# Small rows of w_up: ten DMA engines and three column blocks instead of eight engines and two and a half

## The chip, the cores and the metric

The kernel runs on one core of a Trainium2 chip. The core has five engines that work side by side: PE (TensorE, matrix products), DVE (VectorE), ACT (ScalarE), POOL (GpSimd) and SP (SyncE, which here only issues loads). Sixteen DMA engines move data between the chip's memory (HBM) and the core's on-chip memory (SBUF, 128 partitions). The metric is the device time of one execution in microseconds; lower is better.

## The reference

One token `x` of 512 elements goes through two branches, and a gate mixes them. Everything is bf16.

```
q   = x @ wq                      # 32 heads of 128
k,v = the last 4096 of 65536 cached positions, 8 heads, each used by 4 query heads
a   = softmax(q k^T / sqrt(128)) v @ wo
u   = x @ w_up ; gt = x @ w_gate  # both 512 x 1792
b   = (sigmoid(gt) * u) @ w_down  # 1792 x 512
g   = sigmoid(sum(x * gate_w))
out = g * a + (1 - g) * b
```

There is little arithmetic for each byte: the weights and the used part of the caches are 30.67 MB and each byte is read once.

## The kernel before

All large loads are issued by SP, in one queue and in the order of the code: wq (4 MB), eight loads of K (1 MB each, L122), w_gate (L132), w_up (L138 and L144), eight loads of V (L122), two of wo and four of w_down (L109). Up to eight loads are open at a time: a load takes over the semaphore of the one eight places earlier and waits until that one has landed. V loads also wait for the buffers of K, which DVE frees by transposing K (L230). A load is cut into packets that are shared out among DMA engines; each engine adds one to the load's semaphore when its share has landed, and whoever needs the data waits for all of them.

The compute follows the loads. PE projects q (L242), computes the scores S_ps from the transposed K (L269), multiplies w_gate (`glu(0, wg_sb)`), then V by the softmax weights (L344), then w_up (`glu(1, wu_sb)`), then wo and, as the last pieces of w_down come in, w_down (`add_row`, L335). The result row is copied to SBUF by DVE and ACT (L392, L393) and stored (L394). The order on PE, DVE and ACT from L219 on is the order of the code; before that a scheduler sets it.

w_up is a 512 x 1792 matrix. The tile wu_sb puts four consecutive rows (`c` = 0 to 3) on each of the 128 partitions. The main load brings for each partition all but the last FX elements of its four rows. These last elements, of the row `c` = 3, are what this case is about: the "small rows". They are loaded a second way, into the tile wx_sb, by four loads with another shape (L144), so that their 128 packets of 2240 bytes fall on other engines than the rest does:

```python
FX = 5 * FQ // 2          # 1120 columns of the 1792; FQ = 448
wx_v = B_w_up.rearrange("(h b j i c) f -> h b i j c f", h=2, b=2, j=4, i=8)[:, :, :, :, DC - 1, F - FX:F]
```

Each of the four loads brings 32 rows, from a source of 8 by 4 rows. As the small rows lie on other partitions than wu_sb's, the multiplication needs the matching elements of x in the same order. DVE picks them out of the row xr into xp (L195), PE turns xp into a column (xx_ps, L197), and DVE copies it to xx (L202). In `glu(1)` the columns that the main load lacks are then added by two matmuls for each block of columns, one for each half `h` of the small rows (L288).

Of the kernel before, what the change touches and what calls it, by code (L numbers as in the profile page):

```python
# [14 lines left out]
BF16 = mybir.dt.bfloat16  # L15
F32 = mybir.dt.float32
# [3 lines left out]
def kernel(  # L20
# [14 lines left out]
    nc = tc.nc  # L35

    P = 128
    D = A_x.shape[-1]
    DC = D // P
# [8 lines left out]
    F = B_w_gate.shape[1]  # L48
# [3 lines left out]
    FQ = F // 4  # L52
# [12 lines left out]
    const = ctx.enter_context(tc.tile_pool(name="const", bufs=1))  # L65
# [7 lines left out]
    ps_m = ctx.enter_context(tc.tile_pool(name="ps_m", bufs=2, space=bass.MemoryType.PSUM))  # L73

    gap = const.tile([1, 8], F32, name="gap")
    nc.gpsimd.memset(gap[:], 0.0)
    xr = const.tile([1, 2, D], BF16, name="xr")
    nc.scalar.dma_start(xr[:, 0, :], A_x[0, :, :])  # L80
    nc.scalar.dma_start(xr[:, 1, :], gate_w.rearrange("(o n) -> o n", o=1))
# [1 line left out]
    dq = nc.sync  # L83
# [43 lines left out]
    for a in range(HP):  # L127
# [4 lines left out]
    i = dq.dma_start(wg_sb[:].rearrange("p c f -> p (c f)"), B_w_gate.rearrange("(p c) f -> p (c f)", c=DC))  # L132
    reads[i.ins.name] = ((4 * DC * F, P // 4), (1, 4 * DC * F))
    wu_sb = w14.tile([P, DC, F], BF16, name="wu_sb", tag="w14")

    FX = 5 * FQ // 2
    LM = DC * F - FX
    dq.dma_start(wu_sb[:].rearrange("p c f -> p (c f)")[:, 0:LM],  # L138
                 B_w_up.rearrange("(p c) f -> p (c f)", c=DC)[:, 0:LM])
    wx_sb = const.tile([64, 2, 3 * FQ], BF16, name="wx_sb")  # L140
    wx_v = B_w_up.rearrange("(h b j i c) f -> h b i j c f", h=2, b=2, j=4, i=8)[:, :, :, :, DC - 1, F - FX:F]
    for h in range(2):
        for b in range(2):
            dq.dma_start(wx_sb[32 * b:32 * b + 32, h, 0:FX], wx_v[h, b])  # L144

    vv = []
    for a in range(HP):
# [41 lines left out]
    for c in range(DC):  # L189
        nc.tensor.matmul(xt_ps[:, c:c + 1], lhsT=xr[:, 0, c:D:DC], rhs=ident[0:1, 0:1],  # L190
                         start=True, stop=True, skip_group_check=True)
    xx_ps = ps_m.tile([64, 2], F32, name="xx_ps", tag="m")
    xp = const.tile([1, 2, 64], BF16, name="xp")
    for h in range(2):
        nc.vector.tensor_copy(xp[:, h, :].rearrange("o (b i j) -> o b i j", b=2, j=4),  # L195
                              xr[:, 0, :].rearrange("o (h b j i c) -> o h b i j c", h=2, b=2, j=4, i=8)[:, h, :, :, :, DC - 1])
        nc.tensor.matmul(xx_ps[:, h:h + 1], lhsT=xp[:, h, :], rhs=ident[0:1, 0:1],  # L197
                         start=True, stop=True, skip_group_check=True)
    xT = const.tile([P, DC], BF16, name="xT")
    nc.vector.tensor_copy(xT[:], xt_ps[:])  # L200
    xx = const.tile([64, 2], BF16, name="xx")
    nc.vector.tensor_copy(xx[:], xx_ps[:])  # L202


# [18 lines left out]
    for u in range(4):  # L223
        nc.tensor.matmul(S_ps[u // 2][:, u % 2, :], lhsT=other[:].rearrange("p o y u -> p (o y u)"),  # L224
                         rhs=ident[0:2, 0:2].rearrange("p (o y) -> p o y", o=1).to_broadcast([2, 256, 2]),
                         start=True, stop=False)
# [11 lines left out]
    for k in range(8):  # L238
        q_ps = ps_big.tile([P, 512], F32, name="q_ps", tag="b")
        ks = slice(k * 512, (k + 1) * 512)  # L240
        for c in range(DC):
            nc.tensor.matmul(q_ps[:], lhsT=xT[:, c:c + 1].to_broadcast([P, P]),  # L242
                             rhs=wq_sb[:, c, ks], start=(c == 0), stop=(c == DC - 1))
# [18 lines left out]
    for a in range(HP):  # L262
        for v in range(2):
            kT = kTs[a, v] if (a, v) in kTs else k_transpose(a, v)
            k_v = kT[:].rearrange("p (n dhi s t) -> p n dhi s t", n=KB, dhi=2, s=32)
            for dhi in range(2):
                for t in range(2):
                    for hb in range(2):
                        nc.tensor.matmul(S_ps[v][:, hb, :], lhsT=q_st[:, a, dhi, :, t],  # L269
                                         rhs=k_v[:, hb * 16:(hb + 1) * 16, dhi, :, t],  # L270
                                         start=False, stop=(a == HP - 1 and dhi == 1 and t == 1))
# [4 lines left out]
    def glu(w, wsb):  # L276
        for c in range(DC):
            for j in range(4):
                g_out = gu_ps[w][32 * j:32 * j + 32, 0:FQ]

                f0, f1 = j * FQ, (j + 1) * FQ
                fm = min(max(F - FX, f0), f1) if w == 1 and c == DC - 1 else f1
                if fm > f0:
                    nc.tensor.matmul(g_out[:, 0:fm - f0], lhsT=xT[:, c:c + 1].to_broadcast([P, 32]),  # L284
                                     rhs=wsb[:, c, f0:fm], start=(c == 0), stop=(c == DC - 1 and fm == f1))
                if fm < f1:
                    for h in range(2):
                        nc.tensor.matmul(g_out[:, fm - f0:FQ], lhsT=xx[:, h:h + 1].to_broadcast([64, 32]),  # L288
                                         rhs=wx_sb[:, h, fm - (F - FX):f1 - (F - FX)], start=False, stop=(h == 1))


    pm2 = work.tile([P, 2], F32, name="pm2")
    for v in range(2):
        nc.vector.tensor_reduce(pm2[:, v:v + 1], S_ps[v][:].rearrange("p a b -> p (a b)"), axis=AX.X, op=ALU.max)  # L294
    pm = work.tile([P, 1], F32, name="pm")
    nc.vector.tensor_tensor(pm[:], pm2[:, 0:1], pm2[:, 1:2], op=ALU.max)
    glu(0, wg_sb)
    sge = work.tile([P, FQ], F32, name="sge")
    nc.scalar.activation(sge[:], gu_ps[0][:, 0:FQ], AF.Exp, scale=-1.0)  # L299
# [7 lines left out]
                     start=True, stop=True)  # L307
# [34 lines left out]
    for a in range(HP):  # L342
        for m in range(NP // 4):
            nc.tensor.matmul(pv_ps[32 * a:32 * a + 32, :, :],  # L344
                             lhsT=eT[:, a, 4 * m:4 * m + 4, :].rearrange("p n r -> p (n r)"),
                             rhs=vv[a][:, 4 * m:4 * m + 4, :],
                             start=(m == 0), stop=(m == NP // 4 - 1))
# [7 lines left out]


    glu(1, wu_sb)

    o_ps = ps_m.tile([P, HQ], F32, name="o_ps", tag="m")
# [7 lines left out]
    for u in range(2):  # L367
        for t in range(2):
            nc.tensor.matmul(oY_ps[:, 16 * u:16 * u + 16], lhsT=perm[:, u, t, :], rhs=oX[:, 16 * t:16 * t + 16],
                             start=(t == 0), stop=(t == 1))  # L370
# [54 lines left out]
```

## Time and profile before

| what | value |
|---|---|
| median of 7 times | 79.62 us (79.38 to 80.76) |
| the seven times | 79.60, 79.73, 79.49, 80.75, 79.38, 79.62, 80.76 us |
| profiled execution | 79.53 us, of which span 77.9 us |
| PE busy | 51.9 us (67%) |
| DVE busy | 38.3 us (49%) |
| ACT, POOL busy | 10.9 us, 4.6 us |
| mean TensorE clock granted | 0.976 |
| read from HBM | 30.67 MB, 394 GB/s over the span |
| small loads wx_sb | four, 70 KB each, issued 20.3 to 27.6 us |
| `glu(1)` on PE | w_up matmuls 63.6 to 65.3 us, small rows 65.1 to 65.7 us |

The profile gives for every engine its busy time, and for idle time what ended it. A load is followed from its issue to its landing. The "chain that ended last" goes back from the last instruction to what released it, step by step; the DMA view gives the packets of a stretch of time by queue, and a table of stages gives, for chosen stretches, busy time and count of each engine, the granted clock, the mean share of time in which the 16 DMA engines were busy, and GB/s. Beside these views the trace holds every single DMA packet with start, length and size (without the engine's number), and the time of every increment of a load's semaphore.

### The profile page before, as it was taken

The page shows a single profiled execution, that of the slowest core. Times are in us where ns is not written, and L with a number is a line of the kernel's source. Part 1 is how long each engine was busy: PE and PEld are TensorE (multiplying, and loading weights), DVE is VectorE, ACT ScalarE, POOL GpSimd, SP SyncE. Part 2 cuts the span into 40 slices and gives each one's busy share as a digit, 9 for nine tenths or more (in the row PEclk, how much of TensorE's full clock was granted, in tenths as well). Part 3 has the DMA queues.
Part 4 walks back from the last instruction along what each step waited for, and adds up shares of the span by engine and source line. Part 5 has one row for each costly group of instructions (what it writes and reads, how often), then busy time and mean ns, then how long its engine had stood idle before and what let it go on. Part 6 is the DMA issues. An engine that isn't in the chain of part 4 may idle for free.

```text
span 77.9 us, 823 instructions
## 1 busy us (share of the span) xinstructions
PE 51.9 (67%) x318; PEld 23.8 (31%) x318; DVE 38.3 (49%) x49; ACT 10.9 (14%) x20; POOL 4.6 (6%) x18
## 2 busy tenths in 40 slices
PE   0100092999914788988889305999997699576760
PEld 0200041344402233333332202335442244455520
DVE  0600900029959999999995429983000000591020
ACT  2400000337742000000000293000000003000010
POOL 7940020000000000000000000000000000000000
PEclk9999999999999999999999995599999999999999
DMA  5889799898997989996999979989799897998600
GB/s 152 303 353 505 337 505 454 353 505 353 488 471 337 539 353 454 471 471 273 422 500 412 522 303 522 438 370 522 303 522 438 370 522 320 497 438 358 284 32 1
DMA packets 1624, 30.71 MB, mean 394 GB/s; under 512 B 435, under 2 KB 438, under 8 KB 598
## 3 DMA queue, kind: packets, MB, share of 16 engines
q1 hardware_dynamic: 1616, 30.67, 92.6%
q8 instruction: 2, 0.03, 0.2%
q10 hardware_dynamic: 6, 0.00, 0.0%
HBM read 30.67 MB, written 0.00 MB: 394 GB/s over the span
## 4 chain that ended last, share of the span: by engine, by line
DMA 93%; SPq 2%; PE 1%; DVE 1%; issue 0%
DMA wu_sb<-in_B_w_up_dram 30%; DMA wd_sb<-in_B_w_down_dram 27%; DMA kn<-in_A_k_cache_dram 21%; DMA vv<-in_A_v_cache_dram 15%; SPq L122 1%; PE a_ps L335 1%; DVE res L392 1%; SPq L115 0%
## 5 line engine op out<-in xcount | busy, mean ns | idle before, releaser
L269 PE MATMUL S_ps<-kT,qbig 128*128 128x512 bf16 x64 | 15.2, 378 | 5.0 <-DVE qbig L258 2.8
L344 PE MATMUL pv_ps<-vv,eT 128*32 128x512 bf16 x64 | 15.5, 404 | 4.0 <-DVE eT L316 2.8
L230 DVE STREAM_TRANSPOSE kT<-kn 128x2048 f32<-128x2048 f32 x8 | 17.8, 2282 | 0.2 <-DMA kn<-in_A_k_cache_dram 0.2
L269 PEld LDWEIGHTS <-qbig 128*128 128x128 bf16 x64 | 6.1, 97 | 14.1 <-issue 4.2
L344 PEld LDWEIGHTS <-eT 128*32 128x32 bf16 x64 | 6.2, 102 | 12.5 <-issue 3.4
L242 PE MATMUL q_ps<-wq_sb,xT 128*128 128x512 bf16 x32 | 8.6, 436 | 1.4 <-DMA wq_sb<-in_A_wq_dram 1.4
L363 DVE TENSOR_TENSOR oT<-o_ps,rb 128x32 bf16<-128x32 f32 x1 | 0.2, 192 | 13.2 <-PE o_ps L361 13.2
L247 DVE STREAM_TRANSPOSE qtT<-q_sb 128x512 f32<-128x512 f32 x4 | 2.7, 691 | 6.8 <-ACT q_sb L244 6.8
L224 PE MATMUL S_ps<-ident,other 2*128 2x512 bf16 x4 | 2.0, 610 | 5.6 <-DVE other L182 5.6
L244 ACT CAST q_sb<-q_ps 128x512 bf16<-128x512 f32 x8 | 4.7, 586 | 7.0 <-PE q_ps L242 7.0
L242 PEld LDWEIGHTS <-xT 128*128 128x128 bf16 x32 | 3.5, 110 | 6.8 <-issue 4.1
L335 PE MATMUL a_ps<-wo_sb,oY 128*1 128x256 bf16 x64 | 3.8, 272 | 1.3 <-DMA wo_sb<-in_A_wo_dram 1.0
L335 PEld LDWEIGHTS <-oY 128*1 128x1 bf16 x64 | 2.7, 83 | 2.2 <-issue 1.2
L316 DVE STREAM_TRANSPOSE eT<-e_sb 128x1024 bf16<-128x1024 bf16 x2 | 2.4, 1224 | 1.9 <-ACT e_sb L314 1.9
L299 ACT ACTIVATE sge<-gu_ps 128x448 f32<-128x448 f32 x1 | 0.5, 544 | 18.9 <-PE gu_ps L284 18.9
L354 ACT COPY pv_sb<-pv_ps 128x512 f32<-128x512 f32 x1 | 0.6, 586 | 17.3 <-PE pv_ps L344 17.3
L326 DVE RECIPROCAL sg<-sge 128x448 f32<-128x448 f32 x1 | 3.0, 2953 | 0.0
L294 DVE TENSOR_REDUCE pm<-S_ps 128x1 f32<-128x1024 f32 x2 | 2.4, 1208 | 0.9 <-PE S_ps L269 0.9
L392 DVE CAST res<-a_ps 1x256 bf16<-1x256 f32 x1 | 0.4, 413 | 4.9 <-PE a_ps L335 4.9
L207 DVE TENSOR_TENSOR gpr<-xr 1x512 f32<-1x512 bf16 x1 | 0.7, 680 | 4.4 <-DMA xr<-in_gate_w_dram 4.4
L190 PE MATMUL xt_ps<-ident,xr 1*128 1x1 bf16 x4 | 0.3, 165 | 3.5 <-POOL ident L165 3.5
L335 PE MATMUL a_ps<-wd_sb,hT 128*1 128x256 bf16 x28 | 2.0, 271 | 0.7 <-DMA wd_sb<-in_B_w_down_dram 0.5
(64 smaller groups left out, 32.2 us busy)
## 6 DMA issues: line engine op xcount, KB each, us to landing
kn<-in_A_k_cache_dram SPq DMA_DIRECT2D x8, 1024.0 KB, 16.1
vv<-in_A_v_cache_dram SPq DMA_DIRECT2D x8, 1024.0 KB, 12.2
wq_sb<-in_A_wq_dram SPq DMA_DIRECT2D x1, 4096.0 KB, 12.3
wo_sb<-in_A_wo_dram SPq DMA_DIRECT2D x2, 2048.0 KB, 21.3
wg_sb<-in_B_w_gate_dram SPq DMA_DIRECT2D x1, 1792.0 KB, 21.2
wu_sb<-in_B_w_up_dram SPq DMA_DIRECT2D x1, 1512.0 KB, 23.5
wd_sb<-in_B_w_down_dram SPq DMA_DIRECT2D x1, 1024.0 KB, 24.2
wd_sb<-in_B_w_down_dram SPq DMA_DIRECT2D x1, 384.0 KB, 22.7
```

What stands on the lines that cost most here:

```text
L224: nc.tensor.matmul(S_ps[u // 2][:, u % 2, :], lhsT=other[:].rearrange("p o y u -> p (o y u)"), rhs=ident[0:2, 0:2].rearrange("p (o y) -> p ...
L230: nc.vector.transpose(t[:].bitcast(F32), kn[a][:, v * KB:(v + 1) * KB, :] .rearrange("p n d -> p (n d)").bitcast(F32))
L242: nc.tensor.matmul(q_ps[:], lhsT=xT[:, c:c + 1].to_broadcast([P, P]), rhs=wq_sb[:, c, ks], start=(c == 0), stop=(c == DC - 1))
L244: nc.scalar.copy(q_sb[:, ks], q_ps[:])
L247: nc.vector.transpose(qtT[:].bitcast(F32)[:, kq], q_sb[:].bitcast(F32)[:, kq])
L269: nc.tensor.matmul(S_ps[v][:, hb, :], lhsT=q_st[:, a, dhi, :, t], rhs=k_v[:, hb * 16:(hb + 1) * 16, dhi, :, t], start=False, stop=(a == HP ...
L294: nc.vector.tensor_reduce(pm2[:, v:v + 1], S_ps[v][:].rearrange("p a b -> p (a b)"), axis=AX.X, op=ALU.max)
L316: nc.vector.transpose(eT[:, :, v * KB:(v + 1) * KB, :].rearrange("p a n r -> p n a r"), e_sb[:, v, :].rearrange("p (n a r) -> p n a r", a= ...
L326: nc.vector.reciprocal(sg[:], sge[:])
L335: nc.tensor.matmul(a_ps[32 * i:32 * i + 1, i, 0:HN], lhsT=lhsT, rhs=rhs[:, i * HN:(i + 1) * HN], start=start, stop=stop)
L344: nc.tensor.matmul(pv_ps[32 * a:32 * a + 32, :, :], lhsT=eT[:, a, 4 * m:4 * m + 4, :].rearrange("p n r -> p (n r)"), rhs=vv[a][:, 4 * m:4 ...
L392: nc.vector.tensor_copy(res[:, 0:HN], a_ps[0:1, 0, 0:HN])
```

## The change

The small rows become three whole blocks of columns (1344 columns, 2688 bytes a row). The main load becomes shorter to match: 5824 elements a partition for 6048. The four small loads bring 30, 30, 30 and 40 rows, from sources of 10 by 3 and 10 by 4 rows. These are 130 rows: rows 88 and 89 are loaded twice, and their elements of x in the second place are set to zero. wx_sb has 70 partitions for 64; the first half uses 60 of them. The picking of x is now done by DVE (two copies) and POOL (one copy and two memsets), and the two matmuls that turn xp wait for both. In `glu(1)` the block `j` = 0 of `c` = 3 comes whole from wu_sb and the other three from wx_sb: 19 matmuls for 20. The memset of the unused tile `gap` on POOL is taken out.

```diff
-    gap = const.tile([1, 8], F32, name="gap")
-    nc.gpsimd.memset(gap[:], 0.0)
...
-    FX = 5 * FQ // 2
+    WX_PARTS = [(0, 0, 0, 3), (0, 30, 30, 3), (1, 0, 60, 3), (1, 30, 88, 4)]
+    WX_N = [60, 70]
+    FX = 3 * FQ
     LM = DC * F - FX
     dq.dma_start(wu_sb[:].rearrange("p c f -> p (c f)")[:, 0:LM],
                  B_w_up.rearrange("(p c) f -> p (c f)", c=DC)[:, 0:LM])
-    wx_sb = const.tile([64, 2, 3 * FQ], BF16, name="wx_sb")
-    wx_v = B_w_up.rearrange("(h b j i c) f -> h b i j c f", h=2, b=2, j=4, i=8)[:, :, :, :, DC - 1, F - FX:F]
-    for h in range(2):
-        for b in range(2):
-            dq.dma_start(wx_sb[32 * b:32 * b + 32, h, 0:FX], wx_v[h, b])
+    wx_sb = const.tile([70, 2, FX], BF16, name="wx_sb")
+    for h, p0, e0, r in WX_PARTS:
+        dq.dma_start(wx_sb[p0:p0 + 10 * r, h, :], B_w_up[DC * e0:DC * (e0 + 10 * r), :]
+                     .rearrange("(j i c) f -> i j c f", j=r, i=10)[:, :, DC - 1, F - FX:F])
...
-    xx_ps = ps_m.tile([64, 2], F32, name="xx_ps", tag="m")
-    xp = const.tile([1, 2, 64], BF16, name="xp")
+    xx_ps = ps_m.tile([70, 2], F32, name="xx_ps", tag="m")
+    xp = const.tile([1, 2, 70], BF16, name="xp")
+    nc.gpsimd.memset(xp[:, 0, WX_N[0]:WX_N[1]], 0.0)
+    nc.vector.tensor_copy(xp[:, 0, 0:WX_N[0]].rearrange("o (b i j) -> o b i j", b=2, j=3),
+                          xr[:, 0, 0:DC * WX_N[0]].rearrange("o (b j i c) -> o b i j c", b=2, j=3, i=10)[:, :, :, :, DC - 1])
+    for (h, p0, e0, r), eng in zip(WX_PARTS[2:], (nc.gpsimd, nc.vector)):
+        eng.tensor_copy(xp[:, h, p0:p0 + 10 * r].rearrange("o (i j) -> o i j", j=r),
+                        xr[:, 0, DC * e0:DC * (e0 + 10 * r)].rearrange("o (j i c) -> o i j c", j=r, i=10)[:, :, :, DC - 1])
+
+    nc.gpsimd.memset(xp[:, 1, 30:38].rearrange("o (i j) -> o i j", j=4)[:, :, 0], 0.0)
     for h in range(2):
-        nc.vector.tensor_copy(xp[:, h, :].rearrange("o (b i j) -> o b i j", b=2, j=4),
-                              xr[:, 0, :].rearrange("o (h b j i c) -> o h b i j c", h=2, b=2, j=4, i=8)[:, h, :, :, :, DC - 1])
         nc.tensor.matmul(xx_ps[:, h:h + 1], lhsT=xp[:, h, :], rhs=ident[0:1, 0:1],
                          start=True, stop=True, skip_group_check=True)
...
-                f0, f1 = j * FQ, (j + 1) * FQ
-                fm = min(max(F - FX, f0), f1) if w == 1 and c == DC - 1 else f1
-                if fm > f0:
-                    nc.tensor.matmul(g_out[:, 0:fm - f0], lhsT=xT[:, c:c + 1].to_broadcast([P, 32]),
-                                     rhs=wsb[:, c, f0:fm], start=(c == 0), stop=(c == DC - 1 and fm == f1))
-                if fm < f1:
-                    for h in range(2):
-                        nc.tensor.matmul(g_out[:, fm - f0:FQ], lhsT=xx[:, h:h + 1].to_broadcast([64, 32]),
-                                         rhs=wx_sb[:, h, fm - (F - FX):f1 - (F - FX)], start=False, stop=(h == 1))
+                if w == 1 and c == DC - 1 and j >= 1:
+                    for h, n in enumerate(WX_N):
+                        nc.tensor.matmul(g_out, lhsT=xx[0:n, h:h + 1].to_broadcast([n, 32]),
+                                         rhs=wx_sb[0:n, h, (j - 1) * FQ:j * FQ], start=False, stop=(h == 1))
+                    continue
+                nc.tensor.matmul(g_out, lhsT=xT[:, c:c + 1].to_broadcast([P, 32]),
+                                 rhs=wsb[:, c, j * FQ:(j + 1) * FQ], start=(c == 0), stop=(c == DC - 1))
```

In the built program SP still issues four small loads between w_up and V. On POOL, the two memsets and the copy stand after `spare` and before the copies of `perm`. On PE, the two matmuls of xp now stand behind the first matmul of L224, which waits for DVE.

More of the change, by code (lines that the diff above doesn't have):

```diff
@@ L200 @@
     nc.vector.tensor_copy(xT[:], xt_ps[:])
-    xx = const.tile([64, 2], BF16, name="xx")
+    xx = const.tile([70, 2], BF16, name="xx")
     nc.vector.tensor_copy(xx[:], xx_ps[:])
```

## The prediction

> **What bounds the kernel now.** I read the whole page first, then the chain that ended last, the DMA view whole and in two windows, the tiles wu_sb and wx_sb, a table of stages over the end, and the trace's single records: every DMA packet with start, length and size, and every increment that a load makes on its semaphore.
>
> Queues of the whole span (packets, MB, share of 16 engines' time), then the chain by line:
>
> ```profile
> q1 hardware_dynamic: 1616, 30.67, 92.6%
> q8 instruction: 2, 0.03, 0.2%
> ...
> DMA wu_sb<-in_B_w_up_dram 30%; DMA wd_sb<-in_B_w_down_dram 27%; DMA kn<-in_A_k_cache_dram 21%; DMA vv<-in_A_v_cache_dram 15%; SPq L122 1%; PE a_ps L335 1%; DVE res L392 1%; SPq L115 0%
> ```
>
> The load queue is full for 92.6% of the span and carries 93% of the chain. So the question is when the last of the 16 DMA engines finishes its share. The second line will matter: two packets that are no data. The same view in windows 39 to 40.1 us and 67.4 to 68.6 us:
>
> ```profile
> q8 instruction: 1, 0.02, 5.5%
> ...
> q8 instruction: 1, 0.02, 5.1%
> ```
>
> Each is one packet of 16384 bytes, 0.96 and 0.98 us long, on one engine (5.5% of 16 x 1.1 us = 0.97 us).
>
> The end, by stages (last two columns: mean DMA share, GB/s), and the chain there (start, length, what):
>
> ```profile
> 72.80:73.30 0.50, 0.14 (x4) 0.11 (x5) 0.00 (x0) 0.00 (x0) 0.00 (x0) 1.00 0.67 279
> 73.30:74.10 0.80, 0.80 (x18) 0.59 (x16) 0.00 (x0) 0.00 (x0) 0.00 (x0) 1.00 0.53 220
> 74.10:74.70 0.60, 0.48 (x8) 0.24 (x6) 0.00 (x0) 0.00 (x0) 0.00 (x0) 1.00 0.16 62
> ...
> 53.73 20.93 DMA wd_sb<-in_B_w_down_dram
> 74.66 0.04 issue
> 74.70 0.64 PE a_ps L335 x6
> 75.34 0.40 DVE res L392
> ```
>
> The engines do not finish together. The last w_down load makes its 16 increments at 73.15 to 73.65 us (six engines) and at 74.47 to 74.98 us (ten). From 74.98 the tail is fixed: last matmul, copy of res until 75.74, output store, span 77.9; 79.53 with what lies around it, against a median of 79.62 over seven times.
>
> Who are the ten? On each engine one packet starts within 5 ns of the end of the one before, so packets can be strung into 16 chains. A 32768-byte packet takes 1.213 us on every one, so the chains keep the offsets they had when the first load ended (12.09 to 12.69 us). From there to the last packet: six "plain" chains 60.56 us; eight "carriers", which have the small w_up rows, 62.02; two hit by an instruction packet 62.10. So the small rows cost a carrier 1.46 us (sixteen 2240-byte packets of 91 ns, four increments of 9 ns, 0.03 of overlaps) and an instruction packet costs its engine 1.54, of which the trace shows 0.96 to 0.98 for itself and 0.47 to 0.50 more in the data packet after it. The two fall on different engines, and neither is a carrier. In finish times: carriers 74.12 to 74.62, hit engines 74.40 and 74.53, plain 72.80 to 73.29. The kernel is balanced by this: eight engines carry extra so that two hit ones need not.
>
> **What the change does to each kind of engine.**
> 1. Main load of w_up, 11648 for 12096 bytes a partition, eight a partition group, all 16 engines. From 8192 bytes in 309 ns and 12096 in 453 the slope is 0.0369 ns a byte: 16.5 ns less a packet, -0.13 us on every engine.
> 2. Small rows on a carrier: 13 packets of 2688 bytes. From 2240 bytes in 91 ns and 4096 in 159: 107.4 ns. 13 x 107.4 + 4 x 9 - 0.03 = 1.40 us for 1.46. With step 1 an old carrier changes by -0.13 - 0.06 = -0.19.
> 3. Two engines newly carry: -0.13 + 1.40 = +1.27. The number of carriers is the first dimension that both sides share: now 32 rows from 8 by 4 and eight increments a load (the trace counts eight and one immediate); then 30 or 40 rows from 10 by 3 or 4, so ten.
> 4. Other engines: -0.13.
>
> Sum if the two new carriers are plain ones: they end at 72.80..73.29 + 1.27 = 74.07..74.56, old carriers at 74.43, hit engines at 74.27 and 74.40. The last end moves from 74.62 to between 74.43 and 74.56: -0.19 to -0.06 us. If a new carrier is the engine hit at 67.55: 74.53 + 1.27 = 75.80, or +1.18 us; if it is the one hit at 39.07: 74.40 + 1.27 = 75.67, +1.05. Everything behind waits along: the last w_down piece, six matmuls, res, store.
>
> **Which engines are they?** The trace numbers no engines, and this is the unknown that decides. By chance, two of the eight non-carriers miss both hit ones in 15 of 28 pairs. But the first packets of the first load start in an order: seven of eight carriers at 1.759 to 1.846 us, one at 1.901, the non-carriers at 1.885, 1.961, 1.969, 1.986, 1.994, 1.995, 1.998, 2.688. (Two chains that touch within 4 ns are told apart by the lone gate_w packet, which I take to be on a carrier.) Halves so cleanly ordered suggest the engines are started in sequence. The chain that starts at 1.885 is the one hit at 67.55; the one at 1.969 is the one hit at 39.07. If ten engines are the first ten of that sequence, the new carriers are 1.885 and 1.961 or near them: a hit engine among them. I put this at 0.58.
>
> The row: ten-engine loads are not in this trace; eight-engine ones are. [...] The row again: each instruction packet cost its engine 1.54 us here. [...]
>
> **Small steps, and what hides them.**
> - Start: gap's memset leaves (0.10 us), two POOL memsets (0.09 to 0.10 each by spare and gap) and a POOL copy of 30 elements come (between 0.26, the perm copies, and 1.28, DVE's slower xp copy). They stand after spare (ends 3.97) and before the four perm copies, which nobody needs until 67. The DVE xp copies, two of 1.2 us overlapping to 1.32, stay about that.
> - The second wait: both xx matmuls now wait for POOL and are queued behind the first "other" matmul (9.56, 0.60). So xx comes some 0.9 us later, z_ps behind it 0.3 later, then gex and gg; two xx matmuls 0.26. PE's next work, q_ps, waits until 13.06 for wq, after PE stood idle 1.38 us. Hidden; without that cover 0.3 us.
> - glu(1): 19 matmuls for 20, six of them on 60 or 70 rows. At most 0.2 us of PE less at 65, before idle waits of 1.04 (wo) and 0.53 (wd). Nothing.
> - SP: still four small loads. Later V loads reuse their semaphores; a fetch-hit carrier would land them at 41.30 + 1.40 = 42.70 instead of 41.62, while three V loads stay queued until 48.88. Nothing, or below 0.1.
>
> **The rivals.**
> - A, forecast: a hit engine becomes a carrier, +1.05 to +1.18, at the latest chain offset (12.69 for 12.44) +1.43. 79.62 + 1.13 = 80.75. For it: start order. Against: order inside a half may be chance.
> - B, other side: both new carriers are plain. -0.06 to -0.19; 79.43 to 79.56, take 79.48, within 0.3%. It decides as soon as both hit engines are outside the ten. The hit pair then ends last or nearly so. A gain over 0.3% (0.24 us, about what a measurement of this kernel can tell from no change) needs chain offsets luckier than this run's by 0.05 or more: I give that a fourth of B.
> - C: the hit engines differ between executions. Two of the seven times are 80.75 and 80.76, what an instruction packet on a carrier would give (62.02 + 1.54 for the chain, some +1.1 to +1.5). Ten carriers of 16 are then hit more often than eight, and a median falls in the upper or the lower group. No third time comes from it; it raises A against chance, and I count it in A and B.
> - D: the load runs on fewer engines than ten. On five, 26 packets are 2.83 us: carriers +1.24, and 80.9. Price much like A; 0.02.
>
> **How the numbers follow.** A and D 0.60; B 0.40, of which 0.10 beyond 0.3%. The time is A's: 80.75, A's own range 80.5 to 81.05. Both cases must be in the range: 79.38 (B's better end less a little of run-to-run spread) to 81.05 (79.62 + 1.43). Between the two groups I expect little.
>
> **What would show it.** Right in A: last w_down load's increments with one or two alone, over 1 us after the rest; a chain with both a 16384-byte packet and thirteen 2688-byte ones; 107 and 437 ns for the new packets; the six matmuls of the tail starting near 75.9. Right in B: four increments near 73.1 to 73.5, twelve within 74.2 to 74.95. Wrong in both: a last increment later than 76.5, or PE waiting for xx before 13 us. The prediction falls if both instruction packets stay on engines that carry nothing.

## The result, and the profile after

The changed kernel takes 81.21 us as a median of 24 times (79.85 to 82.04), the kernel before 79.63 us over 59 (79.30 to 81.07). The ratio is 1.0088, with a 95% interval of 1.0069 to 1.0106: slower, by less than one per cent. The times of both kernels fall into groups, and the ratio leaves out what lies over 1.5% above a kernel's fastest time, which is 13 of the changed kernel's 24 and its profiled execution too; the plain medians stand at 1.020.

Sorted, the times of the changed kernel are 79.85, 79.86, 79.94; eight from 80.28 to 80.71; nine from 81.18 to 81.49; four from 81.77 to 82.04. Of the kernel before, 14 of 59 lie over 80.5 and the rest within 79.3 to 80.1. The profiled execution of the changed kernel is one of the nine: 81.36 us, span 79.7 (before: 79.53 and 77.9), so its span has 1.8 us to account for.

The chain of waits of the changed kernel, its end (start, length, what):

```profile
64.68 0.58 PE gu_ps L290 x3
65.26 1.75 PE gu_ps L287 x6
67.01 1.02 PE o_ps L363 x8
...
69.08 8.08 PE a_ps L337 x92
77.16 0.40 DVE res L394
```

Before, this chain ended with a w_down load. Now its last 12 us hold no load: they go from the six matmuls of the small rows by way of short steps on DVE to all 92 matmuls of wo and w_down. In this execution PE became the bound. Its page shows the queues and the granted clock (40 slices of 2 us):

```profile
q1 hardware_dynamic: 1626, 30.68, 90.9%
q8 instruction: 2, 0.03, 0.2%
...
PEclk9999999999999999999999995699999999555699
```

The bytes (but for two rows loaded twice) and the two instruction packets are as before. The row PEclk has a stretch of halves in slices 25 and 26, as before, and a new one in slices 35 to 38, where wo is multiplied; single records put that at 68.13 to 74.96 us. Before, halves stood at 46.9 to 50.3 us and from 77.6 on. The table of stages of both (us; busy time of PE, PEld, DVE, ACT, POOL; granted clock; DMA share; GB/s), first the changed kernel, then the one before:

```profile
68.00:75.00 7.00, 6.19 (x63) 3.84 (x63) 3.22 (x8) 0.00 (x0) 0.00 (x0) 0.51 0.76 318
75.00:77.20 2.20, 2.12 (x39) 1.47 (x34) 0.05 (x1) 0.01 (x1) 0.00 (x0) 1.00 0.00 0
```

```profile
68.00:75.00 7.00, 5.30 (x90) 3.72 (x85) 2.36 (x5) 0.00 (x0) 0.00 (x0) 1.00 0.73 309
75.00:77.20 2.20, 0.30 (x4) 0.08 (x1) 0.41 (x1) 0.36 (x1) 0.00 (x0) 1.00 0.00 0
```

In the same seven microseconds PE gets through 63 matmuls at clock 0.51 where it did 90 at 1.00, and works another 2.1 us with no load left (DMA share 0.00).

The timeline of PE in both, the changed kernel first (start, length, what, idle time before it and its releaser):

```profile
65.19 0.09 PEld L287 LDWEIGHTS <-xx 60*32 60x32 bf16 x1 [0.37 <-issue]
65.19 1.82 PE L287 MATMUL gu_ps<-wx_sb,xx 60*32 60x448 bf16 x6
65.48 0.09 PEld L287 LDWEIGHTS <-xx 70*32 70x32 bf16 x1 [0.20 <-issue]
65.77 0.09 PEld L287 LDWEIGHTS <-xx 60*32 60x32 bf16 x1 [0.20 <-issue]
...
69.08 6.51 PE L337 MATMUL a_ps<-wo_sb,oY 128*1 128x256 bf16 x64 [0.28 <-DVE oY L374]
75.42 1.69 PE L337 MATMUL a_ps<-wd_sb,hT 128*1 128x256 bf16 x28
```

```profile
65.14 0.12 PEld L288 LDWEIGHTS <-xx 64*32 64x32 bf16 x6 [0.37 <-issue]
65.14 0.56 PE L288 MATMUL gu_ps<-wx_sb,xx 64*32 64x224 bf16 x6
67.77 1.91 PE L335 MATMUL a_ps<-wo_sb,oY 128*1 128x256 bf16 x32 [0.28 <-DVE oY L372]
70.72 1.91 PE L335 MATMUL a_ps<-wo_sb,oY 128*1 128x256 bf16 x32 [1.04 <-DMA wo_sb<-in_A_wo_dram]
73.16 2.13 PE L335 MATMUL a_ps<-wd_sb,hT 128*1 128x256 bf16 x28 [0.53 <-DMA wd_sb<-in_B_w_down_dram]
```

Two things changed ahead of the half clock. The six small-row matmuls take 1.82 us for 0.56. A single one is no longer than before (0.36 us, at most 0.36 before), but before, all six weight loads ran within 0.12 us and the matmuls overlapped. Now, at each change between 60 and 70 rows, the next weight load (PEld) starts only 0.20 us after the end of the last, and the matmuls run one after another. So wo begins at 69.08 for 67.77, 1.31 us later, and the idle waits of 1.04 and 0.53 us, in which PE stood waiting for loads (its slack), are gone.

The loads moved too, by less. From the single packet records, strung into chains as in the prediction, with the order of the loads kept on each chain (time from the end of an engine's first load to its last packet, us; a carrier has its small rows on top of the share of all other loads that every engine has):

```
                      before   predicted after   measured after
carriers              62.02    61.82             62.25
plain engines         60.60 *  60.44             60.90
last packet ends      74.62                      74.85
last increments       73.15 to 73.65 (six)       73.41 to 73.83 (four)
                      74.47 to 74.98 (ten)       74.73 to 75.22 (twelve)
* the prediction has 60.56; 60.60 less 0.13 is 60.47
```

Twelve late and four early: ten carriers and the two engines with an instruction packet, at 39.67 and 67.83 us, that carry nothing. No increment comes alone over 1 us after the rest. So the forecast's mechanism did not occur in this execution; but every engine, carrier or not, is some 0.43 us later than these sums. The new packets have the predicted lengths (11648 bytes 436 ns; 2688 bytes 107 ns) for the first five to eight small packets of a carrier; then nearly all take 133 to 176 ns, on all carriers together. The first V packets beside them (32768 bytes, from the next loads in the queue) take 0.05 to 0.37 us more than their 1.213, on all 16 engines. I call this contention below. Some 0.06 us is left: from V on, packets are 1 to 6 ns longer each, for which I have no cause.

### The profile page after: what moved, and what is told of

It reads as the page before. It is cut to its first block, busy times and chain, and to the rows that moved or that the text cites. A ratio compares the mean times of both kernels' runs of the same rounds, so it can differ in the third digit from the quotient of the medians.

```text
span 79.7 us, 823 instructions
## 1 busy us (share of the span) xinstructions
PE 55.7 (70%) x317; PEld 25.4 (32%) x317; DVE 38.4 (48%) x49; ACT 10.9 (14%) x20; POOL 4.7 (6%) x20
## 4 chain that ended last, share of the span: by engine, by line
DMA 50%; PE 22%; DVE 14%; issue 6%; SPq 5%; DVEq 0%
DMA kn<-in_A_k_cache_dram 29%; DMA vv<-in_A_v_cache_dram 21%; DVE kT L235 11%; PE a_ps L337 10%; PE pv_ps L346 5%; SPq L119 4%; PE S_ps L274 2%; PE gu_ps L287 2%; DVE pm L296 2%; PE o_ps L363 1%; PE gu_ps L290 1%; DVE res L394 1%; SPq L112 0%; PE oY_ps L371 0%; DVE oX L367 0%
## 5 line engine op out<-in xcount | busy, mean ns | idle before, releaser
L337 PE MATMUL a_ps<-wo_sb,oY 128*1 128x256 bf16 x64 | 6.5, 396 | 0.3 <-DVE oY L374 0.3
L337 PEld LDWEIGHTS <-oY 128*1 128x1 bf16 x64 | 3.9, 119 | 2.7 <-DVE oY L374 0.4
L229 PEld LDWEIGHTS <-other 2*128 2x128 bf16 x4 | 0.6, 157 | 6.1 <-DVE other L181 5.9
```

Of the source, the lines that this page charges most:

```text
L337: nc.tensor.matmul(a_ps[32 * i:32 * i + 1, i, 0:HN], lhsT=lhsT, rhs=rhs[:, i * HN:(i + 1) * HN], start=start, stop=stop)
```

## The experiments

Two causes show in the profile, alternation of 60 and 70 rows on PE and contention among ten carriers; a third, an instruction packet on a carrier, may be at work in other executions. Ratios are to the kernel before, run beside each. In all of them the output is still the whole result.

**Without the alternation.** In the changed kernel both halves use 70 rows, the ten spare ones of the first half zeroed:

```diff
+    nc.gpsimd.memset(wx_sb[:, 0, :], 0.0)
...
-                    for h, n in enumerate(WX_N):
+                    for h, n in enumerate((70, 70)):
```

> The changed kernel with one edit: both halves of the small rows are multiplied over 70 partitions (the ten more of the first half are zeros), where the changed kernel alternates 60 and 70. Theory 'alternation': the 0.20 us that PE loses ahead of each of the six matmuls on wx_sb goes, they take about 0.6 us instead of 1.82, wo's first matmul starts near 67.8 instead of 69.08 us, and the time falls from 81.2 to 79.8-80.1. Theory 'hit carrier' (the prediction's): no change, 81.2. The loads are untouched: 2688-byte packets still up to 0.06 us over their 107-109 ns, last increment 75.1-75.3 us unless an instruction packet meets a carrier.

Measured 79.94 us over six times (79.77 to 81.64), ratio 1.0040 (1.0020 to 1.0059). Timeline of PE and the end of its chain:

```profile
65.39 0.55 PE L288 MATMUL gu_ps<-wx_sb,xx 70*32 70x448 bf16 x2
...
68.00 5.42 PE L338 MATMUL a_ps<-wo_sb,oY 128*1 128x256 bf16 x64 [0.28 <-DVE oY L375]
73.59 2.09 PE L338 MATMUL a_ps<-wd_sb,hT 128*1 128x256 bf16 x28 [0.17 <-DMA wd_sb<-in_B_w_down_dram]
```

```profile
54.09 20.97 DMA wd_sb<-in_B_w_down_dram
75.07 0.04 issue
75.11 0.61 PE a_ps L338 x6
75.72 0.40 DVE res L395
```

The gaps are gone, the matmuls overlap again (they mix with those over 128 rows), wo starts at 68.00, and the chain ends with a load again. A half clock came here too (68.5 to 71.9 us, wo takes 5.42 us), but PE had the slack for it and still waits 0.17 us for w_down. Alternation is therefore shown as one part. The rest of the loss stays: small packets with a median of 150 ns, chains of 62.52 us (carriers) and 61.17 (plain), last increment 75.36 us for 74.98.

**One matmul of 128 rows, loads at 0, 40, 80 and 120.** This takes the alternation away as well and moves the rows to other partitions (the matching edits of xp, xx and the matmuls are left out here):

```diff
+    wx_sb = const.tile([P, FX], BF16, name="wx_sb")
+    for h in range(3):
+        dq.dma_start(wx_sb[40 * h:40 * h + 40, :], B_w_up[DC * 40 * h:DC * 40 * (h + 1), :]
+                     .rearrange("(j i c) f -> i j c f", j=4, i=10)[:, :, DC - 1, F - FX:F])
+    dq.dma_start(wx_sb[120:P, :], B_w_up[DC * 120:DC * P, :].rearrange("(i c) f -> i c f", c=DC)[:, DC - 1, F - FX:F])
```

> The changed kernel with the 128 small rows in one block of 128 partitions: loads of 40, 40, 40 and 8 rows (10 by 4 three times, then 8) to partitions 0, 40, 80 and 120, so that each engine's four rows lie in a group of four partitions that starts at a multiple of four, no row is loaded twice, and one matmul of 128 rows serves each block of columns. Theory 'shared partition groups' for the slow packets: 2688-byte packets at 107-109 ns without excess, V packets beside them at 1.213 us, last increment 74.7-74.9; with PE's alternation gone as well, 79.4-79.6 us. Rival 'source rows' (ten engines reading rows 140 KB apart): packets keep an excess of 0.03-0.06 us and neighbours of 0.1-0.4 us, last increment 75.1-75.3, 79.8-79.9.

Measured 81.37 us, ratio 1.0219 (1.0184 to 1.0254), far over both expectations. Small packets took up to 0.29 us, the first V packets 0.2 to 0.9 us more, and the 32768-byte packets of V and wo had medians of 1225 and 1227 ns for 1213, of which nothing had warned me. The last increments end in one at 77.09 and one at 77.84 us, alone: in this execution two carriers were hit by instruction packets. The run tells no cause apart, but it shows two new ones.

**The alternation alone, and a shift of the rows alone,** both in the kernel before. The first gives the second half six zeroed rows (64 and 70 rows in turn); the second puts the rows on partitions 2 to 65, multiplied over 66 rows. Of each edit the main lines:

```diff
-                        nc.tensor.matmul(g_out[:, fm - f0:FQ], lhsT=xx[:, h:h + 1].to_broadcast([64, 32]),
-                                         rhs=wx_sb[:, h, fm - (F - FX):f1 - (F - FX)], start=False, stop=(h == 1))
+                        nc.tensor.matmul(g_out[:, fm - f0:FQ], lhsT=xx[0:64 + 6 * h, h:h + 1].to_broadcast([64 + 6 * h, 32]),
+                                         rhs=wx_sb[0:64 + 6 * h, h, fm - (F - FX):f1 - (F - FX)], start=False, stop=(h == 1))
```

```diff
-            dq.dma_start(wx_sb[32 * b:32 * b + 32, h, 0:FX], wx_v[h, b])
+            dq.dma_start(wx_sb[2 + 32 * b:34 + 32 * b, h, 0:FX], wx_v[h, b])
```

> The kernel before with one edit: the second half of its small rows is multiplied over 70 partitions (six of zeros), the first over 64 as it was; loads as before. Theory 'alternation': the six matmuls on wx_sb take 1.5-1.9 us instead of 0.56, wo's first matmul starts 1.0-1.3 us later than 67.77, and the PE slack of 1.04 + 0.53 us is mostly gone: at full clock the time stays near 79.6-79.8, and wherever the clock is halved near the end it is 80.5-81.5; the mean over the executions rises. Theory 'hit carrier': no change, 79.6.

> The kernel before with one edit: the small rows lie two partitions further up (2 to 65 instead of 0 to 63, two partitions of zeros below), so that an engine's four rows reach over two groups of four partitions; the rows read, the eight engines and the packet size stay. Theory 'shared partition groups': 2240-byte packets over 91 ns (100-140), V packets beside them longer, last increment 75.1-75.4, 79.8-80.0 us. Rival 'source rows': packets at 91 ns, no change, 79.6.

Measured 80.41 us, 1.0102 (1.0077 to 1.0126), and 80.77 us, 1.0151 (1.0120 to 1.0183). Neither can be read as meant: in both, the 32768-byte packets of V and wo had a median of 1225 ns for 1213, and w_gate's 57344-byte packets 2148 for 2116. What they share is that a larger xp pushes every later tile 32 bytes on.

**Only the addresses.** The tile `gap` (32 bytes) and its memset are taken out of the kernel before, and nothing else. The changed kernel also loses `gap`, but its xp grows by as much, so its large tiles stay where they were.

```diff
-    gap = const.tile([1, 8], F32, name="gap")
-    nc.gpsimd.memset(gap[:], 0.0)
```

> The kernel before with one part of the change alone: the unused tile gap (32 bytes a partition) and its memset are taken out. In the built program this puts wq_sb, kn, wg_sb, wu_sb, vv, wo_sb and wd_sb at addresses that are 32 over a multiple of 64, where before, and in the changed kernel, they are multiples of 64. The first runs of alternate, shift and aligned had these tiles at 32 over as well, and their 32768-byte packets had a median of 1224-1225 ns for 1213. Theory 'address': packets of 32768 bytes 1225 ns, of 57344 bytes 2148 (2116), last increment 75.6-75.9, 80.3-80.5 us. Rival (the longer packets came from the other edits, or from the chip): 1213 ns, 79.6 us.

Measured 80.48 us (80.36 to 80.57), ratio 1.0125 (1.0103 to 1.0147). The page's queue lines:

```profile
DMA packets 1624, 30.71 MB, mean 389 GB/s; under 512 B 435, under 2 KB 438, under 8 KB 598
...
q1 hardware_dynamic: 1616, 30.67, 92.1%
```

The packets are as many as before; V packets take 1225 ns for 1213 and w_gate's 2148 for 2116, and the last increment comes at 76.02 us for 74.98. An unused tile of 32 bytes is worth 1.25%. The expectation's "multiples of 64" turned out too weak, as the later runs showed. In the fourteen kernels of this case, wherever wq_sb and the tiles after it start at a multiple of 512 bytes, V packets have a median of 1213 or 1214 ns (eight kernels: before, after, both halves over 70 rows, alternation and shift once more below, both marked ones, and the last one below). Where the tiles start 32, 320, 352, 384 or 480 bytes past a multiple of 512 (the other six), it is 1222 to 1226. No kernel had them 256 past one, so whether multiples of 256 would do is not shown. Not every load is touched: wq and K, loaded first, have medians of 1213 in all fourteen, and w_up's main packets their old lengths (436 ns, or 453 and 454) in all but this one (465). Why the offset matters, and why not to those loads, stays open.

**Alternation and shift again, with the tiles in place.** The two edits above with `gap` taken out.

> alternate without the tile gap, so that the large tiles lie at multiples of 64 again as in the kernel before: only the matmuls over 64 and 70 partitions in turn are left as a difference. Theory 'alternation': the six matmuls take 1.6 us instead of 0.56, PE starts wo about 1.1 us later, packets 1213 ns, last increment 74.9-75.1; 79.5-79.8 us where PE runs at full clock after 67 us, 80.2-81.5 where it does not; the fast ones 0 to 0.6% over before. Rival (alternation costs nothing; all of alternate's 1.0% was the address): same as before within 0.2%.

> shift without the tile gap, so that the large tiles lie at multiples of 64 again: only the small rows' partitions (2 to 65 for 0 to 63) are left as a difference. Theory 'shared partition groups': 2240-byte packets at a mean of 93-96 ns for 91, V packets next to them 0.05-0.13 us longer, together 0.1-0.2 us per engine; last increment 75.1-75.2, 79.75-79.9 us. Rival 'source rows': 91 ns, 79.6 us.

The alternation measured 79.83 us, ratio 1.0030 (1.0007 to 1.0053). Timeline of PE in its profiled execution (80.84 us):

```profile
66.35 1.63 PE L288 MATMUL gu_ps<-wx_sb,xx 64*32 64x224 bf16 x6
...
70.06 5.03 PE L335 MATMUL a_ps<-wo_sb,oY 128*1 128x256 bf16 x64 [0.28 <-DVE oY L372]
74.92 1.70 PE L335 MATMUL a_ps<-wd_sb,hT 128*1 128x256 bf16 x28
```

The six matmuls take 1.63 us for 0.56 in a kernel whose loads are the old ones: the price of the alternation by itself. By the single records, the weight load behind a matmul of 224 columns waits 0.11 us, behind one of 448 columns 0.20. So a change had no one price in this run: the wait is longer behind the longer matmul (0.27 us with 224 columns, 0.36 with 448). In the run over 70 rows, where the six stand among matmuls of 128 rows, their weight loads wait 0.2 us in all; in the changed kernel, over 60 and 70 rows in turn, they wait 1.4 (0.37 of it ahead of the first). What makes them wait is not shown.

The fastest two of the ten times, 79.44 and 79.49 us, are level with the kernel before.

The profiled execution held a second thing. Its last increments are at 73.05 to 73.61 us (eight), 74.43 to 74.97 (six), and 75.90 and 76.19 alone. Both instruction packets fell on carriers, and those two ended 0.9 to 1.2 us after the other carriers. From first load to last packet they took 63.48 and 63.53 us, the other carriers 62.01. The mechanism of the forecast exists, in some executions, and already with eight carriers.

The shift measured 79.88 us, ratio 1.0051 (1.0033 to 1.0069). In its trace (79.51 us) small packets took 91 ns without excess and the first V packets 0.03 to 0.05 us more (0.19 once); the chains are 0.09 us longer than before (62.10 and 60.69), and the last increment came at 74.95. The trace is of the fastest of the eight times; the next five lie at 79.81 to 79.93. So the half per cent of the others is not in the one trace there is, and stays open.

**Where ten carriers contend.** Ten engines, four rows of each load for each of them, at partitions 0 to 39 and then at 32 to 71 (that an engine's four rows are neighbours is my reading of the 10 by 4 source; the records of packets have no partition); the eight rows left go to every fourth partition of the others, and three matmuls of 72 rows replace the two for each block of columns (no alternation). The loads alone:

```diff
+    nc.gpsimd.memset(wx_sb[:], 0.0)
+    for h in range(3):
+        dq.dma_start(wx_sb[0:40, h, :], B_w_up[DC * 40 * h:DC * 40 * (h + 1), :]
+                     .rearrange("(j i c) f -> i j c f", j=4, i=10)[:, :, DC - 1, F - FX:F])
+    dq.dma_start(wx_sb[40:72:4, 0, :], B_w_up[DC * 120:DC * P, :].rearrange("(i c) f -> i c f", c=DC)[:, DC - 1, F - FX:F])
```

> The changed kernel's ten engines, but each load of 40 rows goes to partitions 0 to 39 (three column slots side by side) and the last eight rows to every fourth partition from 40 to 68, so that the four rows of an engine lie in one group of four that begins at a multiple of four; all matmuls on them over 72 partitions (no alternation); large tiles at multiples of 64. Theory 'shared partition groups': packets near 107-110 ns, V neighbours with at most half of the changed kernel's excess, last increment 74.8-75.0, 79.45-79.65 us. Rival 'source rows' (ten readers 140 KB apart): excess as in the changed kernel, last increment 75.1-75.4, 79.8-80.0 us.

```diff
-        dq.dma_start(wx_sb[0:40, h, :], B_w_up[DC * 40 * h:DC * 40 * (h + 1), :]
+        dq.dma_start(wx_sb[32:72, h, :], B_w_up[DC * 40 * h:DC * 40 * (h + 1), :]
-    dq.dma_start(wx_sb[40:72:4, 0, :], B_w_up[DC * 120:DC * P, :].rearrange("(i c) f -> i c f", c=DC)[:, DC - 1, F - FX:F])
+    dq.dma_start(wx_sb[0:32:4, 0, :], B_w_up[DC * 120:DC * P, :].rearrange("(i c) f -> i c f", c=DC)[:, DC - 1, F - FX:F])
```

> own_ports with the small rows moved: the three loads of 40 rows go to partitions 32 to 71 for 0 to 39, the last eight rows to every fourth partition from 0 to 28; the large tiles lie at multiples of 128 again (in own_ports they were 64 over, with 1222 ns a packet). Ten engines, source rows, packet size and matmuls stay. [...] Rival 'source rows' or 'ten readers': first six packets at 107 ns, later ones at 140-230, V packets 0.3-0.8 us longer, last increment 75.2-75.7, 79.9-80.4 us.

At 0 to 39: 81.72 us, ratio 1.0284 (1.0226 to 1.0343). At 32 to 71: 80.89 us, 1.0162 (1.0104 to 1.0221). The DMA view of 39.5 to 41.5 us, the first at 0 to 39, the second at 32 to 71:

```profile
DMA packets 168, 0.73 MB, mean 363 GB/s; under 512 B 41, under 2 KB 41, under 8 KB 154
```

```profile
DMA packets 187, 1.01 MB, mean 505 GB/s; under 512 B 47, under 2 KB 47, under 8 KB 164
```

The same loads by the same ten engines move 363 GB/s at the one place and 505 at the other. At 0 to 39 small packets take 107 ns for the first four to eight and then, with few exceptions, 184 to 241 on all carriers, and the first V packets 0.15 to 0.82 us more on all 16 engines. At 32 to 71 small packets take 107 ns (the first of a carrier up to 112), and no V packet is over 0.02 us longer than the rest, but for one behind an instruction packet. So the theory of the first run, that groups of four partitions are enough, fell, and so did source rows and the number of readers as causes: of what was tried, it is the choice of partitions that decides. The changed kernel, whose loads lie at 0 to 69, has slow packets too (133 to 176 ns, V 0.05 to 0.37 us more). Which partitions get in each other's way, and how, no trace shows. What the V packets at 0 to 39 do show is that all 16 engines slow down, also the six that carry no small rows. Both kernels had large tiles off a multiple of 512 bytes (320 and 384), with V packets of 1222 to 1226 ns for 1213, which keeps even the second ratio well over 1.

**Which engines are hit.** To number the engines, seven tiny loads that nothing reads, of 9 to 15 rows and each of another length, are set between the K loads; in both kernels:

```diff
...
+            m = 2 * a + y
+            if marked and m < 7:
+                dq.dma_start(mark[0:9 + m, m, 0:64 + 16 * m], B_w_gate[0:9 + m, 0:64 + 16 * m])
```

> The kernel before with seven tiny loads between the K loads: 9, 10, ... 15 rows of 128, 160, ... 320 bytes into an unused tile. If a load of n rows runs on the first n engines, the sets of engines are nested and each chain's number can be read from the marks that it carries. Theory 'sequence' (the prediction's): the order in which the first packets start is the engines' number, nearly; the two instruction packets fall on engines 8 to 11. Rival 'no order': the first packets' order says nothing within a half. Theory 'moves': the numbers hit differ from those in other executions. Time: up to 0.3 us more, not of interest.

> The changed kernel with the same seven tiny loads. Theory 'fixed': the two instruction packets fall on the engines of the same numbers as in marks_before. Theory 'moves': on others. The carriers are those with the marks of up to 10 rows, engines 0 to 9; packets of 2688 bytes start at 107 ns and rise to 140-170 after the first six or seven, on all carriers together.

Measured 79.73 and 80.08 us, one time each. A load of 9 to 15 rows leaves a packet of its length on that many engines, so the chains can be told apart and are numbered by the marks they carry. Before: the carriers are engines 0 to 7, and the instruction packets are on 11 (39.31 us) and 12 (68.86). First packets of the others start in the order 9, 12, 10, 15, 11, 13, 14, 8. In the changed kernel the carriers are 0 to 9, the instruction packets again on 11 (39.37) and 12 (67.88), and here 11 is the first of all sixteen to start (1.755 us) and 12 the third last (2.380). So the order of starts that I took for engine numbers means nothing within the half, and the engines hit in both marked traces are two that ten carriers do not reach. Of the fourteen traces of this case twelve have both instruction packets on engines that carry nothing, two (the alternation with tiles in place, and the 128-row one) on carriers.

The second run also shows the changed kernel under a full clock until 77.5 us. Its timeline and chain:

```profile
65.62 1.82 PE L292 MATMUL gu_ps<-wx_sb,xx 60*32 60x448 bf16 x6
...
69.50 3.66 PE L342 MATMUL a_ps<-wo_sb,oY 128*1 128x256 bf16 x64 [0.28 <-DVE oY L379]
73.63 2.14 PE L342 MATMUL a_ps<-wd_sb,hT 128*1 128x256 bf16 x28 [0.47 <-DMA wd_sb<-in_B_w_down_dram]
```

```profile
54.22 20.91 DMA wd_sb<-in_B_w_down_dram
75.13 0.04 issue
75.17 0.63 PE a_ps L342 x6
75.81 0.40 DVE res L399
```

The alternation costs its 1.82 us here too, but wo takes 3.66 us for 6.51, PE still waits 0.47 us for w_down, and the last load sets the end, 0.33 us later than in the marked kernel before (75.45 for 75.12, by the last increments). So here the alternation costs nothing at the end; in these traces it does only together with a half clock in the tail.

**All put right.** Rows at partitions 32 to 71, no alternation, and `gap` enlarged so that the large tiles start at multiples of 512 bytes:

```diff
-    gap = const.tile([1, 24], F32, name="gap")
+    gap = const.tile([1, 56], F32, name="gap")
```

> from32 with 128 more bytes of unused tile ahead of the large tiles: wq_sb, kn, wg_sb, wu_sb, vv, wo_sb and wd_sb start at multiples of 512 bytes a partition, as in the kernel before and the changed one; in from32 they were 384 over, in own_ports 320, in no_gap 480, and in all three the packets from w_gate on took 1222-1225 ns for 1213. Theory 'address': V packets 1213 ns, w_gate packets 2116, last increment 74.7-74.9 us, 79.35-79.55 us in executions whose instruction packets miss the carriers, so level with or up to 0.2 us under the kernel before. Rival (the slower packets come with the small rows' new place): 1222 ns, 80.2-80.4 us as in from32. If instruction packets meet the first ten engines more often than the first eight, the upper group (81.0-81.6) holds more than the 3 in 10 that it has before.

Measured 80.14 us over twelve (79.42 to 80.78), ratio 1.0050 (1.0005 to 1.0095). Its chain of waits ends with a load:

```profile
53.47 20.93 DMA wd_sb<-in_B_w_down_dram
74.40 0.04 issue
74.44 0.63 PE a_ps L335 x6
75.07 0.40 DVE res L392
```

In its trace (79.45 us) small packets take 107 ns, V 1213, w_gate 2116; carriers 61.84 us where 61.82 was predicted, plain engines 60.48 for 60.44 (60.47 from the corrected 60.60), last increment 74.71 for 74.98. The prediction's sum of packets holds once nothing contends, and ten carriers as such do not contend. The time does not follow: the time outside the span is 1.95 us here for 1.63 before (1.95 to 2.0 in all three kernels of 72 rows, which start POOL with a memset of 3.45 us), and I have not found why. Six of the times are 79.42 to 79.74 and six 80.53 to 80.78; beside it, before has 12 of 17 at 79.37 to 79.88 and five at 80.68 to 80.96. An upper group of half the times is what ten carriers, hit more often than eight, would give, but no trace of an upper execution of this kernel was taken, so that is argued and not shown. By its ratio it lies between the changed kernel and the kernel before, and its interval overlaps the changed kernel's.

## Why the prediction was right or wrong

Slower was right, by luck: the reason given for it, a hit engine that becomes a carrier, did not occur in either trace of the changed kernel. By the ratio the time is 79.62 x 1.0088 = 80.32 us (80.17 to 80.46), in the range but below A's 80.5 to 81.05; the plain median, 81.21, is above the range. Of the thirteen times over 81 us, the one that was profiled is accounted for; the others are not.

1. Steps 1 to 4, the prices of the packets: right. 436 ns for 436.5, 107 for 107.4, ten carriers (ten increments for a small load, eight before); the sum met its two chains within 0.04 us in the last experiment. One reading was off: the plain engines took 60.60 us and not 60.56, as overlaps of packets come to some 0.07 us on a carrier for the 0.03 assumed. So small rows cost 1.42 us for 1.46 and an instruction packet 1.49 for 1.54, too little to change the forecast. What was missing is a term, put at nothing without a reason: that packets take longer where ten carriers write to partitions 0 to 69 (133 to 176 ns for 107). It is worth some 0.4 us on every engine; with the alternation taken away, 0.40% of the time is left.
2. "Which engines are they?" failed, and with it A, which carried 0.58 of the chances. The inference from start order to engine number has no ground: the marked loads show the hit engines as 11 and 12, and ten carriers as 0 to 9. In both traced executions of the changed kernel the instruction packets stayed on engines that carry nothing, where by its own last line the prediction falls.
3. Rival B had the right engines (four early, twelve late) and the wrong price, for want of the same term.
4. Rival C, that the hit engines differ between executions, is shown by two of fourteen traces, the run of 128 rows and, cleanly, the second alternation run: both instruction packets on carriers, which end 0.9 to 1.2 us after the rest, about the forecast's price. I had folded it into A and B and given it no price of its own. Whether it makes the upper times of the changed kernel is not shown.
5. "glu(1): ... Nothing" failed, and in the profiled execution this is the largest step. I counted matmuls and rows and not that going from 60 to 70 rows and back ends their overlap (1.82 us for 0.56). PE had 1.57 us of slack in two waits; the alternation takes 1.25 to 1.3 of it, and a half clock on wo (2.85 us more in the profiled execution, 6.51 for the 3.66 of the marked one) then makes PE the bound, 2 us after the last load. Taking the alternation out brings 1.0088 down to 1.0040, and adding it to the kernel before gives 1.0030.
6. "Start" was right: the second xx wait is hidden, as the group of q_ps in the changed kernel shows, idle 1.0 us for wq as its last releaser.

```profile
L247 PE MATMUL q_ps<-wq_sb,xT 128*128 128x512 bf16 x32 | 9.0, 452 | 1.0 <-DMA wq_sb<-in_A_wq_dram 1.0
```

7. "Between the two groups I expect little" failed: eight of 24 times lie at 80.28 to 80.71. The parts shown, contention of some 0.4 us, alternation under more or less of a half clock, and now and then a hit carrier, can make such a spread; which of them makes which time is not shown. The mean granted clock that goes with each time narrows it. Every trace of this case has 3.4 us or more of half clock at some point from 46 to 53 us, and 3.4 us alone bring the mean to 0.978 (0.976 in the kernel before, whose tail ran at full clock). Three of the eight, 80.28, 80.30 and 80.34 at 0.973 to 0.978, and two of the thirteen over 81, 81.26 at 0.973 and 81.43 at 0.979, leave no room for a long half clock on wo as well, so there the alternation should have cost nothing, as in the marked run at 0.973. The kernel without alternation also has one time of 81.38 at 0.979, and the kernel before several over 80.5 at 0.973 to 0.978. A hit carrier is the candidate for such times.

## What to carry to other kernels

When a change redistributes packets, cost not only the bytes for each engine but where they land: here, the same loads by ten engines moved 363 GB/s in the same 2 us with the rows at partitions 0 to 39 and 505 at 32 to 71. Count on TensorE the changes of row count too, and not only the matmuls: 60 and 70 rows in turn, or 64 and 70, ended the overlap here (1.82 and 1.63 us for 0.56). Give a stage's slack a price under a half clock before calling it cover: here, 1.57 us of slack met some 1.3 us of alternation and 2.85 of half clock. Hold the addresses of the large tiles fixed when comparing two kernels, or 32 bytes of an unused tile (1.25% here) can outweigh the change under study (0.88%).

## What the runs showed of the hardware that was not expected

- In the six kernels whose large tiles start off a multiple of 512 bytes (32 to 480 past one, 256 not tried), packets of w_gate and of the loads from V on were longer, the large ones by 1% to 3% and w_down's small ones by up to 7%: 1225 ns for 1213, 2148 for 2116, 332 for 309. In the run without `gap`, where nothing else differs, that is 1.25% of the time.
- With ten engines writing to partitions 0 to 39, packets of 107 ns took 184 to 241, and the first V packets on all 16 engines 0.15 to 0.82 us more; at 32 to 71 it was 107 ns (up to 112 for the first of a carrier) and at most 0.02 us.
- Matmuls over 60 and 70, or 64 and 70, contraction rows in turn did not overlap: the next weight load waited 0.11 us behind one of 224 columns and 0.20 us behind one of 448, and six took 1.82 and 1.63 us for 0.56.
- The granted clock fell to a half for 3.4 to 6.8 us in the tail of several executions (68.13 to 74.96 in the changed kernel's), and not in others with the same matmuls (the marked one); what triggers it is not settled here.
- Instruction packets fell on engines 11 and 12 in the two marked traces; in two other traces they fell on engines that carry small rows. One costs its engine some 1.49 us in the kernel before, 0.96 to 0.98 of it for itself.
